# Tiny loads of 15 down to 3 rows behind one large load, in a two-layer decode kernel

## The chip, the core and the metric

The kernel runs on one core of a Trainium2 chip. The metric is the device time of one execution in microseconds (us). Before the change it is 1313.94 us, the median of three runs (1313.61 to 1314.49).

## The reference

Two rounds of the same two layers on an input `x` of 2 batches, 1 token and 448 features: attention against a cache of 4096 keys and values in 16 heads of 256, then a gated layer of 1792.

```
def _A_ref(x, k_cache, v_cache, wq, wo):
    q = heads(x @ wq)                                   # 2 x 16 x 1 x 256
    p = softmax(einsum("bhqd,bhkd->bhqk", q, k_cache) * 256 ** -0.5)
    return merge(einsum("bhqk,bhkd->bhqd", p, v_cache)) @ wo
def _B_ref(x, W_gate, W_up, W_down):
    gate = x @ W_gate; gate = gate * (gate > 0)
    return (gate * (x @ W_up)) @ W_down
x = x + _A_ref(layernorm(x), k_cache, v_cache, wq, wo)
x = x + _B_ref(layernorm(x), W_gate, W_up, W_down)
x = x + _A_ref(layernorm(x), k_cache, v_cache, wq, wo)  # the same caches and weights again
x = x + _B_ref(layernorm(x), W_gate, W_up, W_down)
```

Everything is float32. The keys and values are 134 MB each and are read in both rounds, so the kernel reads 560 MB.

## The kernel before

A *unit* is one pair of head and batch; there are 32, in the order `first` in the first round and `second` (the last four of `first` backwards, then the rest) in the second. For a unit VectorE (DVE) multiplies the 4096 keys with the query (L524) and sums each product (L538); GpSimd (POOL) takes the maximum and the sum over the partitions (L601, L629); ScalarE (ACT) takes the exponentials; TensorE (PE) weighs the values (L659) and projects (L711). Each of the 128 partitions holds 32 keys and 32 values of a unit.

All loads go into one tile, `arena`, which has room for three *blocks* of 64 KB a partition and three single places for weights. In the middle of each round a block is filled by one load of 128 x 16384 floats from `vk` (8.39 MB): the values of one unit and the keys of the next, which lie side by side in memory, 64 KB for each partition. Its size in the code is `n == PAIR`, and `WHOLE_FIRST` and `WHOLE_SECOND` are the positions in the two orders that are loaded so. Other positions are loaded in smaller parts, and between the blocks come pairs of weights (`w_pair`, 1.8 MB).

The list `pending` holds all loads in the order in which they are issued. `release` frees a place when a unit's keys or values have been used, and `pump` then issues from the head of the list whatever finds room. All these loads are issued on SyncE's (SP's) queue by one line (L159 before the change):

```
for i, j in zip(parts, parts[1:]):
    nc.sync.dma_start(dst[:, i:j], src[:, i:j])
```

The waits of each instruction are put in by the framework from the tiles that it reads and writes. Loads signal their landing on eight semaphores, `DMAHW0` to `DMAHW7`, which the loads take in turn; the input `x`, loaded on ACT's queue, has taken the first. SP works through its instructions in order.

Of the kernel before, what the change touches and what calls it, by code (L numbers as in the profile page):

```python
# [8 lines left out]
F32 = mybir.dt.float32  # L9
# [6 lines left out]
P = 128  # L16
# [7 lines left out]
PAIR = 2 * NC  # L24
# [2 lines left out]
KEPT = 20  # L27
ALONE = 25
SPARED = 12
TINY = 174  # L30
KEYS = 8
VALUES = 5
# [48 lines left out]
def two_layers(  # L81
# [10 lines left out]
    nc = tc.nc  # L92
    PSUM = bass.MemoryType.PSUM

    consts = ctx.enter_context(tc.tile_pool(name="consts", bufs=1))
# [20 lines left out]
    def source(key, n):  # L116
        kind, name, c = key
        if kind in "kv":
            h, b = name
            at = (h * B + b + (kind == "v")) % (H * B)  # L120
            if name in spared and n == PAIR:
                return vk[at, :, VALUES * DH : PAIR * UNIT - KEYS * DH]
            size = F if key in left_at else n * UNIT
            c += NC * (kind == "k" and n < PAIR)
            return vk[at, :, c * UNIT : c * UNIT + size]
        if kind == "g":
            return w_pair[name - 1]
        if key in parted:
            at = (kind == "q") * F
            return w_pair[0][:, at : at + F]  # L130
        if kind in "hqo":
            return w_head[weights.index(key)]
        if kind == "in":
            return w_in[:, c * F : (c + n) * F]
        return w_out[:, 14 * P * c : min(14 * P * (c + 1), 14 * D)]

    def pump(by_half=False):
        while pending:
            (kind, name, c), n = pending[0]
            last = at_of.get((kind, name, c - 1)) if kind in "kv" else None  # L140
            if kind == "g":
                last = MIDDLE - (name + 1) % 2
            at = units.take(n, kind, last)
            if at is None:
                return
            pending.pop(0)
            src = source((kind, name, c), n)
            assert at == left_at.get((kind, name, c), at)
            start = place(at) + VALUES * DH * (name in spared and n == PAIR)
            dst = arena[:, start : start + src.shape[1]]  # L150
            parts = [0, src.shape[1]]
            if by_half:
                parts[1:1] = [src.shape[1] // 2]
            if not pending:
                parts[1:1] = [src.shape[1] - CLOSE * TAIL]
            elif len(pending) == 1:
                parts[1:1] = [8 * P]
            for i, j in zip(parts, parts[1:]):
                nc.sync.dma_start(dst[:, i:j], src[:, i:j])  # L159
            for k in range(n):  # L160
                key = (kind, name, c + k)
                if n == PAIR:
                    key = ("k", name, k - NC) if k >= NC else ("v", behind[name], k)
                if kind == "g":
                    key = ("q", name, 0) if (name + k) % 2 == 0 else ("o", name - 1, 0)
                at_of[key] = at + k
                if kind == "in" and k:
                    lies_at[key] = start + k * F
            if n >= NC:
                blocks.add((kind, name))  # L170

    def place(at):
        packed = max(0, at - BLOCKS * PAIR)
        return at * UNIT - packed * (UNIT - F)
# [28 lines left out]
    def release(*key):  # L203
        if key in rest and key not in left_at:
            left_at[key] = at_of[key]
        units.free.add(at_of.pop(key))
        pump(key == ("k", second[0], 0))
# [57 lines left out]
    pending += of_second + [(("in", "", 0), 2)] + [(key, 1) for key in ffn_loads[2:]]  # L265

    tiny = consts.tile([P, TINY], F32, name="tiny")
    tiny_at = {}

    def little(name, *shape, bufs=2):  # L270

        n = 1
        for k in shape:
            n *= k
        if name not in tiny_at:
            start = tiny_at.get(None, 0)
            tiny_at[None] = start + n * bufs
            assert tiny_at[None] <= TINY
            tiny_at[name] = [tiny[:, start + n * i : start + n * (i + 1)] for i in range(bufs)]
        tiny_at[name].append(tiny_at[name].pop(0))  # L280
        found = tiny_at[name][-1]
        if len(shape) == 2:
            found = found.rearrange("p (i j) -> p i j", i=shape[0])
        return found
# [5 lines left out]
    y_end_row = extra[SUMS : SUMS + B, :TAIL]  # L290
    nc.scalar.dma_start(row[:B, :D], x.rearrange("b s d -> (b s) d"))
    pump()


# [5 lines left out]
    rows = little("rows", 4, bufs=1)  # L300
# [110 lines left out]
    def attention(order, after, q_first=None, begun=None):  # L411
# [86 lines left out]
        def score_block(u, c):  # L498
# [6 lines left out]
            there = [(kt, 0)]  # L505
            if order[u] == first[SPARED]:
                most = NT - KEYS
# [132 lines left out]
        def weigh(u, c):  # L640
# [5 lines left out]
            if c == 0:  # L646
                po_of[u] = po[u // 2 % 2]
            held = c == 0 and order[u] == first[SPARED - 1]
            if held and not ahead:
# [85 lines left out]
        for u in range(n_u + 2):  # L735
# [41 lines left out]
            if u == n_u - 1 and aside:  # L777
                units.free.add(slot)
                pump()
# [282 lines left out]
def build(nc, shapes):  # L1062
    import concourse.tile as _tile

    args = [
        nc.dram_tensor(f"in_{n}_dram", s, F32, kind="ExternalInput").ap() for n, s in shapes.items()
    ]
    for i, (shape, _) in enumerate(_OUTS):
        args.append(nc.dram_tensor(f"out_{i}_dram", shape, F32, kind="ExternalOutput").ap())
    with _tile.TileContext(nc) as tc:  # L1070
        two_layers(tc, *args)
# [12 lines left out]
```

## Time and profile before

| | |
|---|---|
| median of three runs | 1313.94 us |
| the profiled execution | 1314.3 us, of it 1312.0 us span |
| DVE busy | 1065.3 us (81%) |
| PE busy | 505.6 us (39%) |
| ACT, POOL busy | 195.2 us (15%), 297.9 us (23%) |
| SP's queue of loads | 560.48 MB, its packets took 99.5% of the time of 16 DMA engines |
| granted TensorE clock, mean | 0.69 |

The span runs from the first to the last instruction. An engine is busy while it computes; the queue of loads is busy while any of its packets is under way on the 16 DMA engines. A wait is put down to the work whose end released it. "SPq" is SP's own sequencer, where a load's row is the time that it takes to issue it, not to move it.

### The profile page before, as it was taken

The numbers are of one execution on the slowest core, as the hardware profiler recorded it, in microseconds if no ns is written. First come the engines' busy times: TensorE is split into PE (matmuls) and PEld (weight loads), VectorE is DVE, ScalarE is ACT, GpSimd is POOL, SyncE is SP. The second block draws the span as 40 slices with busy tenths as digits, with TensorE's granted clock in tenths as the row PEclk, the third lists the DMA queues.
The fourth block names the chain that finished last, engine by engine and source line by source line (L and its number), as shares of the span: only waits on it lengthen the run. The fifth ranks groups of instructions, "written<-read, shape, count | busy, mean of one in ns | idle before, by whom it ended". The sixth has DMA issues, their size and how long they took to land.

```text
span 1312.0 us, 8388 instructions
## 1 busy us (share of the span) xinstructions
PE 505.6 (39%) x3022; PEld 152.0 (12%) x3022; DVE 1065.3 (81%) x711; ACT 195.2 (15%) x789; POOL 297.9 (23%) x169
## 2 busy tenths in 40 slices
PE   3152243332433224324495445322342513433248
PEld 2010010000100001101141101100110100110013
DVE  4988988799897998787619896698999889886892
ACT  1100000010000000122417523000000100012231
POOL 0330412304123040021002151140345304100230
PEclk9665776657766577666697767666676666766669
DMA  9999999999999999999999999999999999999998
GB/s 408 438 432 432 434 426 438 438 426 434 434 430 432 438 432 424 443 420 429 422 399 421 434 427 439 438 436 430 423 443 432 430 430 438 432 432 427 429 421 337
DMA packets 20068, 561.00 MB, mean 428 GB/s; under 512 B 2232, under 2 KB 2364, under 8 KB 6844
## 3 DMA queue, kind: packets, MB, share of 16 engines
q1 hardware_dynamic: 20020, 560.48, 99.5%
q8 instruction: 23, 0.38, 0.1%
q14 instruction: 17, 0.14, 0.0%
q10 hardware_dynamic: 8, 0.00, 0.0%
HBM read 560.47 MB, written 0.00 MB: 427 GB/s over the span
## 4 chain that ended last, share of the span: by engine, by line
DMA 55%; DVE 31%; POOL 7%; PE 4%; issue 2%; ACT 1%; SPq 0%; POOLq 0%; DVEq 0%; ACTq 0%
DMA arena<-in_vk_dram 51%; DVE tiny L538 16%; DVE arena L524 10%; POOL tiny L629 4%; POOL tiny L601 4%; DMA arena<-in_w_in_dram 3%; DVE arena L573 2%; DVE arena L586 2%; DMA arena<-in_w_out_dram 1%; PE small L688 1%; PE po L453 1%; ACT arena L579 1%; DVE row L677 0%; DVE tiny L583 0%; ACT down L617 0%
## 5 line engine op out<-in xcount | busy, mean ns | idle before, releaser
L524 DVE TENSOR_TENSOR arena<-arena 128x8192 f32<-128x8192 f32 (+2 forms) x53 | 450.0, 8492 | 103.4 <-DMA arena<-in_vk_dram 102.6
L538 DVE TENSOR_REDUCE tiny<-arena 128x32 f32<-128x8192 f32 (+1 forms) x54 | 436.5, 8084 | 0.0
L659 PE MATMUL po<-arena,down 128*4 128x512 f32 x2052 | 313.2, 729 | 192.9 <-ACT down L617 116.5
L601 POOL PARTITION_ALL_REDUCE tiny<-tiny x63 | 121.0, 1920 | 719.2 <-DVE tiny L595 718.4
L688 PE MATMUL small<-tiny,row 128*128 128x2 f32 x128 | 30.9, 345 | 558.7 <-DVE row L677 558.7
L629 POOL PARTITION_ALL_REDUCE tiny<-tiny x63 | 149.0, 2364 | 60.4 <-ACT down L617 60.4
L613 ACT ACTIVATE tiny<-tiny 128x1 f32<-128x1 f32 x63 | 18.6, 295 | 734.6 <-POOL tiny L601 734.6
L659 PEld LDWEIGHTS po<-arena,down 128*4 128x4 f32 x2052 | 65.7, 97 | 410.5 <-issue 231.2
L688 PEld LDWEIGHTS small<-tiny,row 128*128 128x128 f32 x128 | 28.1, 306 | 589.1 <-DVE row L677 589.1
L453 PE MATMUL po<-arena,xs 128*33 128x512 f32 (+1 forms) x130 | 65.3, 661 | 0.0
L579 ACT ACTIVATE arena<-arena 128x256 f32<-128x256 f32 x135 | 54.4, 404 | 41.3 <-DVE arena L573 40.4
L711 PE MATMUL acc<-arena,tiny 128*2 128x448 f32 x128 | 51.0, 895 | 21.2 <-DVE tiny L701 21.1
L530 ACT ACTIVATE arena<-arena 128x256 f32<-128x256 f32 x112 | 44.8, 402 | 88.3 <-DVE arena L524 88.3
L465 POOL PARTITION_BROADCAST arena<-arena x32 | 21.8, 749 | 158.5 <-ACT arena L461 147.8
L573 DVE TENSOR_TENSOR arena<-arena 128x1024 f32<-128x1024 f32 (+2 forms) x21 | 32.8, 1560 | 3.4 <-PE acc L711 3.4
L677 DVE SCALAR_TENSOR_TENSOR row<-po,tiny,row 128x256 f32<-128x256 f32 x32 | 15.4, 480 | 22.1 <-ACT row L673 22.0
L461 ACT ACTIVATE arena<-po 33x512 f32<-33x512 f32 x13 | 7.7, 590 | 159.3 <-PE po L453 159.3
L701 DVE TENSOR_TENSOR tiny<-small,tiny 128x4 f32<-128x4 f32 x32 | 5.2, 161 | 28.6 <-PE small L688 28.6
L617 ACT ACTIVATE down<-tiny 128x32 f32<-128x32 f32 x64 | 26.6, 416 | 2.2
L579 ACT ACTIVATION_READ_ACCUMULATOR arena<-arena 128x1 f32 x135 | 25.2, 187 | 0.0
L453 PEld LDWEIGHTS po<-arena,xs 128*33 128x33 f32 x130 | 16.4, 136 | 62.1 <-issue 59.4
L530 ACT ACTIVATION_READ_ACCUMULATOR arena<-arena 128x1 f32 x112 | 21.0, 187 | 0.0
(174 smaller groups left out, 335.8 us busy)
## 6 DMA issues: line engine op xcount, KB each, us to landing
arena<-in_vk_dram SPq DMA_DIRECT2D x17, 4096.0 KB, 38.2
arena<-in_vk_dram SPq DMA_DIRECT2D x16, 2048.0 KB, 32.7
arena<-in_w_pair_dram SPq DMA_DIRECT2D x11, 1792.0 KB, 30.8
arena<-in_vk_dram SPq DMA_DIRECT2D x11, 1024.0 KB, 9.4
arena<-in_w_in_dram SPq DMA_DIRECT2D x12, 896.0 KB, 25.5
arena<-in_vk_dram SPq DMA_DIRECT2D x1, 6528.0 KB
arena<-in_w_head_dram SPq DMA_DIRECT2D x7, 896.0 KB, 22.0
arena<-in_w_out_dram SPq DMA_DIRECT2D x5, 896.0 KB, 19.6
```

What stands on the lines that cost most here:

```text
L453: nc.tensor.matmul(q[:, cols], xs[:, c, :], w_c, start=(i == 0), stop=(i == len(parts) - 1))
L524: nc.vector.tensor_mul(part, part, q_of[u][:, None, :].to_broadcast([P, n, DH]))
L530: nc.scalar.activation(kt[:, t, :], kt[:, t, :], AF.Copy, accum_out=s_of[u][:, t : t + 1])
L538: nc.vector.reduce_sum(found, part, axis=AX.X)
L573: nc.vector.tensor_mul(part[:, :whole, :], kt[:, :whole, :], q_of[u][:, None, :].to_broadcast([P, whole, DH]),)
L579: nc.scalar.activation(part[:, t, :], part[:, t, :], AF.Copy, accum_out=found[:, t : t + 1])
L601: nc.gpsimd.partition_all_reduce(mx_of[u], mx, P, RED.max)
L617: nc.scalar.activation(found, s_of.pop(u).rearrange("p (k r) -> p k r", r=2), AF.Exp, bias=nm, scale=sr[:, b : b + 1], accum_out=rs,)
L629: nc.gpsimd.partition_all_reduce(total[:, b : b + 1], rs, P, RED.add)
L659: nc.tensor.matmul(po_of[u][32 * t : 32 * t + 4, (i - 2 * t) * DH : (j - 2 * t) * DH], p_of[u][:, at : at + 4], values[:, i * DH : j * DH] ...
L688: nc.tensor.matmul(pT_of[u][:, c, :], row[:, c * P : (c + 1) * P], pick[:, b : b + B], start=True, stop=True,)
L711: nc.tensor.matmul(acc[at : at + B], oT_of[h][:, c, :], wo[:, c * D : (c + 1) * D], start=(n < 3), stop=(n >= n_u - 3),)
```

## The change

Behind a load of 128 x 16384 (or, for one unit in the second round, 128 x 13056) whose unit is listed in `STEPPED`, SP issues thirteen more loads. The first reads 15 rows of 13 floats, the next 14 rows of 12 and so on to 4 rows of 2, the last 3 rows of 14. They read the start of what the large load reads, and write side by side into a new tile `steps` of 104 floats a partition, which nothing reads.

```
+STEPS = {rows: rows - 2 if rows > 3 else 14 for rows in range(15, 2, -1)}
+STEPPED = [(2, 0), (6, 0), (10, 0), (13, 0)]
...
             for i, j in zip(parts, parts[1:]):
                 nc.sync.dma_start(dst[:, i:j], src[:, i:j])
+            if n == PAIR and name in STEPPED:
+                stairs(at, src)
...
+    def stairs(at, src):
+        start = 0
+        for rows, n in STEPS.items():
+            nc.sync.dma_start(steps[:rows, start : start + n], src[:rows, :n])
+            start += n
...
+    steps = consts.tile([P, sum(STEPS.values())], F32, name="steps")
```

The four units are loaded whole in the first round; in the second, of the four only (6, 0) and (10, 0) are (positions 16 and 24 of 9 to 28; (2, 0) is at 8 and (13, 0) at 30). That makes six places and 78 added loads: SP's queue has 140 rows before and 218 after. No instruction of another engine is added or moved. As `order` rows from here on, `arena<-in_vk_dram` is a load of keys and values, `DMAHW` are the eight semaphores of landings, and a semaphore named after an engine is that engine's progress.

SP's queue at the first place, the load of unit (2, 0), before. The first row is that load, the next three are the loads of the following units:

```order
L159 DMA arena<-in_vk_dram 128x16384 [waits DMAHW3_49,DVE_49,PE_49]
L159 DMA arena<-in_vk_dram 128x16384 [waits DMAHW0_49,DMAHW4_49,DVE_49,PE_49]
L159 DMA arena<-in_vk_dram 128x16384 [waits DMAHW1_49,DMAHW5_49,DVE_49,PE_49]
L159 DMA arena<-in_vk_dram 128x16384 [waits DMAHW7_49,DVE_49,PE_49]
L159 DMA arena<-in_w_pair_dram 128x3584 [waits PE_49,DMAHW6_49,Activation_49,Pool_49]
```

The same place now, from the same load (it is on `DMAHW7`, as the eighth load of the program) to the next load of a unit:

```order
L161 DMA arena<-in_vk_dram 128x16384 [waits DMAHW3_49,DVE_49,PE_49]
L181 DMA steps<-in_vk_dram 15x13 [waits DMAHW0_49]
...
L181 DMA steps<-in_vk_dram 10x8 [waits DMAHW5_49]
L181 DMA steps<-in_vk_dram 9x7 [waits DMAHW6_49]
L181 DMA steps<-in_vk_dram 8x6 [waits DMAHW7_49]
L181 DMA steps<-in_vk_dram 7x5 [waits DMAHW0_49]
L181 DMA steps<-in_vk_dram 6x4 [waits DMAHW1_49]
L181 DMA steps<-in_vk_dram 5x3 [waits DMAHW2_49]
L181 DMA steps<-in_vk_dram 4x2 [waits DMAHW3_49]
L181 DMA steps<-in_vk_dram 3x14 [waits DMAHW4_49]
L161 DMA arena<-in_vk_dram 128x16384 [waits DMAHW5_49,DVE_49,PE_49]
```

The next unit's load now stands thirteen loads further back, and the eighth tiny load (8x6) waits on the semaphore of the large load ahead of it.

SP's queue at the fifth place, unit (6, 0) in the second round, before:

```order
L159 DMA arena<-in_w_pair_dram 128x3584 [waits DMAHW6_49,PE_49,Pool_49]
L159 DMA arena<-in_vk_dram 128x13056 [waits DMAHW0_49,DVE_49,PE_49]
L159 DMA arena<-in_vk_dram 128x16384 [waits DMAHW1_49,DVE_49,PE_49]
L159 DMA arena<-in_vk_dram 128x16384 [waits DMAHW2_49,DVE_49,PE_49]
L159 DMA arena<-in_vk_dram 128x16384 [waits DMAHW4_49,DVE_49,PE_49]
```

The same place now, from the large load to the next:

```order
L161 DMA arena<-in_vk_dram 128x13056 [waits DMAHW4_49,DVE_49,PE_49]
...
L181 DMA steps<-in_vk_dram 11x9 [waits DMAHW5_49]
L181 DMA steps<-in_vk_dram 10x8 [waits DMAHW6_49]
L181 DMA steps<-in_vk_dram 9x7 [waits DMAHW7_49]
L181 DMA steps<-in_vk_dram 8x6 [waits DMAHW0_49]
L181 DMA steps<-in_vk_dram 7x5 [waits DMAHW1_49]
L181 DMA steps<-in_vk_dram 6x4 [waits DMAHW2_49]
L181 DMA steps<-in_vk_dram 5x3 [waits DMAHW3_49]
L181 DMA steps<-in_vk_dram 4x2 [waits DMAHW4_49]
L181 DMA steps<-in_vk_dram 3x14 [waits DMAHW5_49]
L161 DMA arena<-in_vk_dram 128x16384 [waits DMAHW6_49,DVE_49,PE_49]
```

Here too the eighth tiny load and the large load share a semaphore (the thirteenth, 3x14, and the fifth, 11x9, share `DMAHW5`, so the large load is on `DMAHW0`).

SP's queue near the end of the program, before. This piece is not touched by the change but for the numbers of its semaphores, and it is the place where the trace before shows such a wait by itself:

```order
L159 DMA arena<-in_vk_dram 128x4096 [waits DMAHW2_49]
L159 DMA arena<-in_vk_dram 128x4096 [waits PE_49]
L159 DMA arena<-in_vk_dram 128x4096 [waits DMAHW4_49,PE_49]
L159 DMA arena<-in_vk_dram 128x4096 [waits DMAHW5_49,DVE_49,Activation_49]
L159 DMA arena<-in_vk_dram 128x2048 [waits DMAHW6_49]
L159 DMA arena<-in_vk_dram 128x2048 [waits DMAHW7_49]
L159 DMA arena<-in_w_in_dram 128x3584 [waits DMAHW0_49,PE_49]
L159 DMA arena<-in_w_in_dram 128x1792 [waits DMAHW1_49]
L159 DMA arena<-in_w_in_dram 128x1792 [waits DMAHW2_49,PE_49]
```

The first and the last row are eight loads apart and name the same semaphore.

## The prediction

> **What bounds the kernel now.** I read the page's queues first, then stretches in the middle of the run, then SP's waits.
>
> ```profile
> span 1312.0 us, 8388 instructions
> ...
> GB/s 408 438 432 432 434 426 438 438 426 434 434 430 432 438 432 424 443 420 429 422 399 421 434 427 439 438 436 430 423 443 432 430 430 438 432 432 427 429 421 337
> DMA packets 20068, 561.00 MB, mean 428 GB/s; under 512 B 2232, under 2 KB 2364, under 8 KB 6844
> ...
> q1 hardware_dynamic: 20020, 560.48, 99.5%
> ...
> L524 DVE TENSOR_TENSOR arena<-arena 128x8192 f32<-128x8192 f32 (+2 forms) x53 | 450.0, 8492 | 103.4 <-DMA arena<-in_vk_dram 102.6
> ```
>
> One queue, SP's, is busy for 99.5% of the span. DVE, the busiest engine, still stands idle for 102.6 us ahead of its products, and what ends that is a landing. In the stages with large loads (columns: PE, PEld, DVE, ACT, POOL, then clock, DMA share, GB/s):
>
> ```profile
> 137.00:219.00 82.00, 26.86 (x154) 7.01 (x154) 71.52 (x19) 4.51 (x15) 20.16 (x10) 0.69 1.00 432
> 219.00:300.00 81.00, 29.69 (x156) 7.72 (x156) 71.07 (x20) 8.03 (x21) 20.15 (x10) 0.66 1.00 432
> 300.00:382.00 82.00, 27.57 (x154) 7.29 (x154) 71.18 (x19) 4.51 (x15) 20.56 (x10) 0.67 1.00 432
> ```
>
> The share is 1.00 and the rate 432 GB/s each time. So the loads bound the kernel: a load of 8.39 MB takes 8.39 / 0.432 = 19.4 us, and any time in which the queue is dry is added to the end. What keeps it from running dry is that SP issues early:
>
> ```profile
> 55.80 60.45 SPq L159 DMA_DIRECT2D arena<-in_vk_dram  x4
> DMA to landing us min/median/max: 42.5/42.5/42.5
> 75.00 43.34 DMA arena<-in_vk_dram
> 219.16 70.55 SPq L159 DMA_DIRECT2D arena<-in_vk_dram  x4
> DMA to landing us min/median/max: 43.3/43.3/43.3
> ```
>
> The first row is SP's timeline: the load of unit (2, 0), the first place, is issued at 55.80 us. The second, of that load alone, says that it lands 42.5 us later, at 98.3. The third, from the chain, is the load behind it, issued at 75.00 and landed at 118.3. So the next large load joins the queue 23 us before the one ahead has landed. The last two rows are the same for the second place: issued at 219.16, landed 43.3 us later.
>
> **What a load may wait for.** The added loads need a semaphore each, and the rows of the change name the one that each waits on. That such a wait holds SP until a landing is seen near the end of the run, in the chain and in SP's timeline:
>
> ```profile
> 1231.08 34.98 DMA arena<-in_vk_dram
> 1266.06 0.02 issue
> 1266.08 0.02 SPq L159
> 1266.10 0.03 issue
> 1266.12 28.27 DMA arena<-in_w_in_dram
> ...
> 1230.70 19.85 SPq L159 DMA_DIRECT2D arena<-in_vk_dram  x7
> 1256.34 10.11 SPq L159 DMA_DIRECT2D arena<-in_w_in_dram  x3
> ```
>
> The load issued at 1231.08 lands at 1266.06, and 0.06 us later SP issues another. By the two timeline rows the first is second of seven and the other third of the next three: eight loads later, the pair that shares `DMAHW2` in the order. The later load overwrites nothing of the earlier's; it waits because it takes its semaphore. So a load is not issued before the load eight places ahead of it has landed. With large loads in the middle of the run this costs nothing today: eight of them are over 100 us.
>
> **The change, step by step.** It removes and moves nothing; it adds 78 loads on SP's queue, thirteen at each of six places.
>
> *Tiny loads 1 to 7* wait on the loads ahead of the large one; the seventh waits on the landing of its direct forerunner. They then queue behind the large load. That holds SP some 20 us, but SP only holds up the next load, and see below.
>
> *Tiny load 8* waits on the landing of the large load itself, by both order pieces. SP reaches it long before and stands. When the large load lands, everything issued has landed but the seven tiny ones behind it: the queue is dry. The next large load, which before was under way already, is not yet issued. Its block was free 23 us ago, so it waits for nothing else.
>
> *From the landing to the next data.* SP goes on 0.06 us after the landing (row above). It issues tiny loads 8 to 13, six of them, then the large load. What one issue takes:
>
> ```profile
> 601.90 1.75 SPq L159 DMA_DIRECT2D arena<-in_vk_dram  x4
> L159 SPq DMA_DIRECT2D arena<-in_w_out_dram x10: 327/328/328, 670.8 to 1296.6; - x10
> 0.72 0.53 ACTq L291 DMA_DIRECT2D row<-in_x_dram  x1
> ```
>
> Four issued in a row take 1.75 us, 0.44 each. No row has one of 3 to 15 rows on SP; the nearest are the single issue of 0.33 us and ACT's two-row load of 0.53. I take 0.44, since it is SP's own row with issues back to back; ends 0.33 and 0.53. Six make 2.6 us (2.0 to 3.2). Loads 9 to 13 wait on 1 to 5, which land with the large load or shortly after it, so I count no more for them.
>
> Then the restart: from the issue into a dry queue until data flow. The trace has it at the very start:
>
> ```profile
> DMA to landing us min/median/max: 4.8/4.8/4.8
> ...
> 0.00:2.00 2.00, 0.00 (x0) 0.00 (x0) 0.06 (x1) 0.72 (x1) 0.39 (x5) 1.00 0.23 38
> 2.00:6.00 4.00, 0.00 (x0) 0.00 (x0) 0.00 (x0) 2.51 (x4) 0.00 (x0) 1.00 1.14 424
> ```
>
> The first load, 0.92 MB issued at 0.72 us, lands 4.8 us later; at 432 GB/s its data take 2.1, so the restart cost 2.7. By the stretches, 38 GB/s for 2 us and 424 for 4 moved 1.77 MB by 6.0 us, which is 4.1 us at 432: the restart cost 6.0 - 0.72 - 4.1 = 1.2. I take 2.0, in the middle, since the first way holds the spread of the 16 engines too and the second counts packets that are only begun. Sum for a place: 0.06 + 2.6 + 2.0 = 4.7 us; ends 0.06 + 2.0 + 1.2 = 3.3 and 0.06 + 3.2 + 2.7 = 6.0.
>
> The Trainium skill ("DMA: Bandwidth & Descriptors", Latency and other measured facts) puts the first byte of a load issued by SP at about 600 ns. With 0.6 in place of 2.0 a place would cost 3.3 us and the six 20. The rows above show more, 1.2 to 2.7, and I keep to them.
>
> *The tiny loads' own transfers* I cost at nothing: seven lie at the tail of the large load and six go while SP issues the next, all within the dry time. Without that cover they would be 117 rows of at most 56 bytes a place; no row prices one, but the gap bounds it.
>
> *Afterwards.* The load after next is issued in order right behind. Before, SP issued four loads from 55.80 to about 116 us, one in 20, so that one joined at about 95, shortly ahead of the large load's landing at 98.3; it now comes some 6 us late, into a queue that then holds 19 us of work. The dry time is not made up: the share was 1.00 already. DVE's work stays as it is and waits that much longer. The engines that finish the large load ahead of the others lose that lead too; it costs up to about 1 us in all, and is within the ends.
>
> *Sum.* Six places of 4.7 us are 28 us. The profiled execution took 1314.3 us, 2.3 around its span, and stands 0.4 us above the median of 1313.94, so one base serves both: 1314 + 28 = 1342 us. With the ends, 6 x 3.3 = 20 and 6 x 6.0 = 36: 1334 to 1350.
>
> **Rivals.** A measurement of this kernel can tell about 0.2%, 2.6 us, from no change.
>
> *SP is not held.* If the eighth wait is met by an older landing, or the added loads don't share the eight semaphores as the rows read, SP issues thirteen loads in 13 x 0.44 = 5.7 us, a quarter of its 23 us in hand. The time stays at 1314, or 1 to 2 us more for the transfers. Against it stand the 0.06 us between landing and issue above. For it: that is seen only with small loads. Chance 5%.
>
> *Not slower: the engines fall out of step.* Fewer rows than 16 in a load may reach some of the 16 engines and not others, so the stairs shift the engines against each other. If engines in step hinder one another at the memory, the rate rises afterwards. From 98 us on some 524 MB remain, 1213 us at 432 GB/s; to pay back 28 us the rate must reach 524 / 1.185 = 442 GB/s. At 443, the best slice of the page, the time is 1312. Against it: three stretches at 432 within one unit, and slices of 443 beside others of 420, which rows of 64 KB landing in one slice or the next explain. The Trainium skill (same page and section, on HBM row pitch at large powers of two) has such a rule: copies whose rows lie a large power of two apart fall to half their rate or less, perhaps by streams in step meeting in one channel. Here the pitch is 64 KB, below its cases, and no run here shows a rate that a shift has raised. Chance 3%, of which 2% faster and 1% the same.
>
> *The tiny loads land one after another.* If loads 1 to 5 land only after a restart each, 9 to 13 wait for them in turn: five times 1.2 to 2.7 us more a place, 36 to 81 us in all, 1378 to 1423. Nothing in the trace has a load waiting on a tiny one; but they were issued long before and only queue. Chance 2%.
>
> **How the numbers follow.** The dry queue at six places has 90%. Its ends, 1334 and 1350, come from restart and issue; I widen them by 2 us a side: above for the lead that the engines lose and for tiny loads that land late, below for a restart in mid-run that has less to bring up than the program's first load. The range 1332 to 1352 leaves out the rivals, 10%, and the outermost of its own case. Slower: 90% and the last rival's 2%, 92%. Same: 5% and 1%, 6%. Faster: 2%.
>
> **What would show it.** In the profile after, SP's queue of loads should fall from 99.5% to about 97.5% (28 us of 1340), with a stretch of some 5 us below full share behind each of the six large loads, the first near 98 us. SP should wait on `in_vk_dram` landings for some 20 us at each place, where it waited on DVE before, and its tiny loads should fall into two bunches, seven before the landing and six after, about 0.44 us apart. The next large load should be issued 2.7 us behind the landing and land 24 us behind it, not 20. DVE's idle time ahead of L524 should grow from 102.6 us by about 28. GB/s between the places should stay at 432. The forecast is wrong if SP runs through all thirteen before the landing, if the restart is under 1 or over 3 us, or if the rate between places moves.

## The result and the profile after

The changed kernel takes 1346.75 us, median of four runs (1346.52 to 1347.61), against 1313.91 us for the kernel before, measured beside it: a ratio of 1.0251 with a 95% interval of 1.0233 to 1.0268, 32.8 us slower. The profiled execution has a span of 1344.9 us, 32.9 more than before. In lines of the profile after, numbers of code lines are 2 higher in `pump` and 13 higher in the computation (L524 is now L537).

The page of the changed kernel, its rate by slice, its queue of loads and the wait of DVE ahead of its products:

```profile
span 1344.9 us, 8485 instructions
...
GB/s 409 429 367 437 427 435 437 370 406 443 423 437 398 405 427 437 342 433 432 423 412 421 431 426 439 437 431 435 431 345 437 429 437 430 374 433 431 417 424 350
...
q1 hardware_dynamic: 21424, 560.50, 97.3%
...
L537 DVE TENSOR_TENSOR arena<-arena 128x8192 f32<-128x8192 f32 (+2 forms) x53 | 450.0, 8492 | 140.4 <-DMA arena<-in_vk_dram 133.7
```

The bytes are the same but for 0.02 MB, the queue's share of the 16 engines' time falls from 99.5% to 97.3%, and DVE waits 31 us longer for landings. The rate is not lower everywhere: slices of 367, 370, 398 (with the 405 behind it), 342, 345 and 374 stand where the six places are, and most others are near what they were.

What SP waits for (in total, times, longest), the largest rows of the changed kernel:

```profile
SPq L161 <- DVE tiny L551: 578.6, 40, 35.9
SPq L181 <- DMA arena<-in_vk_dram: 214.7, 13, 19.2
```

SP waits for DVE some 250 us less than the 830.7 of before, and 214.7 us ahead of a tiny load until a load of keys and values lands: the large load of the place or, for the seventh tiny load, the one ahead of it. The first place, in SP's timeline and in the chain that ends with the product of the next unit:

```profile
56.55 0.33 SPq L161 DMA_DIRECT2D arena<-in_vk_dram  x1
...
98.48 1.94 SPq L181 DMA_DIRECT2D steps<-in_vk_dram  x6
100.53 0.83 SPq L161 DMA_DIRECT2D arena<-in_vk_dram  x2
```

```profile
56.55 41.91 DMA arena<-in_vk_dram
98.46 0.02 issue
98.48 0.27 SPq L181
98.75 0.04 issue
98.80 0.29 SPq L181
...
100.53 21.82 DMA arena<-in_vk_dram
122.35 0.02 issue
122.37 8.69 DVE arena L537
```

The large load lands at 98.46. SP issues the six remaining tiny loads from 98.48 on, one in 0.34 us, and at 100.53 the next large load, 25 us later than before. It lands at 122.35: 23.9 us behind the one ahead of it, where a load in a full queue takes 19.4. In between the queue stands dry (DMA share, then GB/s, in the last two columns):

```profile
98.50:100.50 2.00, 2.00 (x24) 0.54 (x24) 1.91 (x1) 0.07 (x1) 1.84 (x1) 1.00 0.03 4
```

### The profile page after: what moved, and what is told of

The parts are those of the page before. It is cut to its first block, busy times and chain, and to the rows that moved or that the text cites. A ratio compares the mean times of both kernels' runs of the same rounds, so it can differ in the third digit from the quotient of the medians.

```text
span 1344.9 us, 8485 instructions
## 1 busy us (share of the span) xinstructions
PE 509.5 (38%) x3022; PEld 154.1 (11%) x3022; DVE 1065.1 (79%) x711; ACT 195.3 (15%) x789; POOL 273.1 (20%) x169
## 3 DMA queue, kind: packets, MB, share of 16 engines
q1 hardware_dynamic: 21424, 560.50, 97.3%
## 4 chain that ended last, share of the span: by engine, by line
DMA 67%; DVE 23%; PE 5%; POOL 2%; issue 1%; ACT 1%; SPq 1%; DVEq 0%; POOLq 0%; ACTq 0%
DMA arena<-in_vk_dram 63%; DVE arena L537 10%; DVE tiny L551 10%; DMA arena<-in_w_in_dram 3%; DVE arena L599 1%; POOL tiny L642 1%; DMA arena<-in_w_out_dram 1%; PE po L466 1%; PE small L701 1%; DVE arena L586 1%; POOL tiny L614 1%; PE po L672 1%; SPq L181 1%; PE acc L724 1%; ACT arena L592 0%
## 5 line engine op out<-in xcount | busy, mean ns | idle before, releaser
L537 DVE TENSOR_TENSOR arena<-arena 128x8192 f32<-128x8192 f32 (+2 forms) x53 | 450.0, 8492 | 140.4 <-DMA arena<-in_vk_dram 133.7
L672 PE MATMUL po<-arena,down 128*4 128x512 f32 x2052 | 317.2, 736 | 186.4 <-ACT down L630 102.3
L614 POOL PARTITION_ALL_REDUCE tiny<-tiny x63 | 95.5, 1516 | 753.1 <-DVE tiny L608 752.5
L642 POOL PARTITION_ALL_REDUCE tiny<-tiny x63 | 149.6, 2374 | 60.4 <-ACT down L630 60.4
L724 PE MATMUL acc<-arena,tiny 128*2 128x448 f32 x128 | 51.1, 895 | 20.8 <-DVE tiny L714 20.7
L478 POOL PARTITION_BROADCAST arena<-arena x32 | 21.8, 749 | 181.0 <-ACT arena L474 170.1
L586 DVE TENSOR_TENSOR arena<-arena 128x1024 f32<-128x1024 f32 (+2 forms) x21 | 32.8, 1560 | 4.2 <-PE acc L724 4.2
```

The costliest lines, as they stand in the source:

```text
L537: nc.vector.tensor_mul(part, part, q_of[u][:, None, :].to_broadcast([P, n, DH]))
L586: nc.vector.tensor_mul(part[:, :whole, :], kt[:, :whole, :], q_of[u][:, None, :].to_broadcast([P, whole, DH]),)
L614: nc.gpsimd.partition_all_reduce(mx_of[u], mx, P, RED.max)
L642: nc.gpsimd.partition_all_reduce(total[:, b : b + 1], rs, P, RED.add)
L672: nc.tensor.matmul(po_of[u][32 * t : 32 * t + 4, (i - 2 * t) * DH : (j - 2 * t) * DH], p_of[u][:, at : at + 4], values[:, i * DH : j * DH] ...
L724: nc.tensor.matmul(acc[at : at + B], oT_of[h][:, c, :], wo[:, c * D : (c + 1) * D], start=(n < 3), stop=(n >= n_u - 3),)
```

## The experiments

All times are against runs of the kernel before on the same chip, whose medians were 1313.75 to 1314.04 us. Where a landing is named without a row, it is read from the trace's landing signals: the trace has 16 of them for each load of 128 rows, which I take to be one from each of the 16 DMA engines, and the last one ends the load.

**Where the wait begins: six tiny loads.** Only the first six of each place are kept:

```
-        for rows, n in STEPS.items():
+        for rows, n in list(STEPS.items())[:6]:
```

> Only the first six tiny loads of each place (15 to 10 rows; 36 of the 78). Theory A (the load that takes the large load's semaphore holds SP until it lands, and the queue runs dry if that load stands ahead of the next large one): the next large load is now the seventh behind and takes the semaphore of the load ahead of the large one, so nothing runs dry: 1314 us, within 2 us of before; queue of loads busy 99.4 to 99.5%. Rival B (each tiny load costs, whatever it waits for): 36/78 of 33 us are 15 us, 1329 us. Rival C (the shift of the engines against each other costs, or the first loads of it): between 1320 and 1347 us.

Measured: 1316.36 us, ratio 1.0019 (1.0010 to 1.0028), queue of loads 99.5% busy. The chain of this run at the first place shows what the next load now waits for:

```profile
40.12 38.91 DMA arena<-in_w_pair_dram
79.04 0.03 SPq L161
79.10 39.72 DMA arena<-in_vk_dram
```

It is the landing of the weights ahead of the large load, at 79.0 us; the load behind is issued 0.1 us later, with the large one still queued in front. Nothing runs dry, as theory A has it. The 2.5 us are slightly more than the 2 allowed. They are not such a wait: behind four of the six places the next load lands 0.25 to 0.33 us further behind the one ahead than in the trace before. Spread over the 36 loads the 2.5 us are 0.07 each, which the queue pays when it has no gap to hide them in (below).

**And one more: seven.** The same edit with `[:7]`.

> One more than in the run of six: the first seven tiny loads (15 to 9 rows; 42 of the 78). Theory A: the next large load is the eighth behind and waits for the large load's landing, so the queue runs dry for wait and restart, without the six issues of 0.34 us: about 0.1 + 2.4 = 2.5 us at each place where the full stairs had 4.6 to 5.5; 15 us and the lost lead of the engines (4 to 5 us in all): 1332 to 1336 us. A step of some 19 us from six to seven loads. Rival B (by the number of loads): 42/78 of 33 us are 18 us, 1332 us, but then six loads give 1329 and the step is 3 us.

Measured: 1334.19 us, ratio 1.0154 (1.0140 to 1.0168). One more load at each place, of 9 rows and 7 floats, costs 17.8 us, where the first six cost 2.5: rival B, a price for each load, falls. The chain at the second place of this run gives the restart by itself, since no tiny load is issued in the gap:

```profile
222.43 43.31 DMA arena<-in_vk_dram
265.75 0.03 SPq L161
265.82 21.88 DMA arena<-in_vk_dram
```

The next load is issued 0.08 us behind the landing and takes 21.9 us, so 2.5 more than in a full queue. And the six issues that distinguish this run from the changed kernel cost 1346.75 - 1334.19 = 12.6 us, 0.35 for each of the 36, which is their spacing in the chain.

**All thirteen, but never against a dry queue.** Six behind the large load, six behind the next load on the queue, one behind the third:

```
             if n == PAIR and name in STEPPED:
-                stairs(at, src)
+                left[:] = list(STEPS.items())
+                begun[0] = 0
+            if left:
+                stairs(src)
...
+        for rows, n in left[:6]:
...
+        del left[:6]
```

> All thirteen tiny loads at each place, but six behind the large load, six behind the next and one behind the one after. Theory A: the load that waits for a landing now has a large load queued ahead of it; the queue does not run dry: 1314 to 1316 us (at the fourth place a small load of weights alone covers the wait, up to 1 us). Rivals B and C (number of loads, or shift of the engines): 1340 to 1347 us, as with the change.

Measured: 1318.91 us, ratio 1.0039 (1.0027 to 1.0052), queue 99.3% busy. The same 78 loads of the same shapes cost 5.0 us instead of 32.8, so neither their number nor a shift of the engines against each other makes the loss. SP's timeline at the first place:

```profile
56.70 0.33 SPq L161 DMA_DIRECT2D arena<-in_vk_dram  x1
57.07 17.69 SPq L186 DMA_DIRECT2D steps<-in_vk_dram  x6
78.82 0.36 SPq L161 DMA_DIRECT2D arena<-in_vk_dram  x1
98.25 2.03 SPq L186 DMA_DIRECT2D steps<-in_vk_dram  x6
100.39 0.35 SPq L161 DMA_DIRECT2D arena<-in_vk_dram  x1
```

Six loads still wait for the large one's landing at 98.2, but the next large load has been issued at 78.8 and flows meanwhile. Only at the fourth place is the cover thin, since the load that flows meanwhile is one of weights of 0.9 MB; the load behind that one comes 0.3 us late. The 5.0 us missed the expectation of up to 2: 78 loads at 0.064 us each on average, about the price with 36. Here the tiny transfers have no gap to hide in.

**More places.** The stairs also behind the unit after each of the four, so that six of seven new places follow directly on an old one:

```
-STEPPED = [(2, 0), (6, 0), (10, 0), (13, 0)]
+STEPPED = [(2, 0), (2, 1), (6, 0), (6, 1), (10, 0), (10, 1), (13, 0), (13, 1)]
```

> The full stairs at thirteen places instead of six: behind the same units and behind the unit after each, in both rounds where these are loaded whole; six of the seven new places are the very next large load, one stands alone. Theory A with the dry queue of 4.6 us at each place and a lost lead that costs only where some time has passed since the last place: 13 x 4.6 = 60 us and 5 to 6 us for the lead: 1379 to 1381 us. Rival D (a place costs 5.5 us wherever it stands, restart and all): 13 x 5.47 = 71 us, 1385 us.

Measured: 1380.79 us, 66.9 more than before, within what theory A gave and 4 us below rival D. DVE's timeline shows the starts of its products, each within 0.15 us of a landing, at the second place and its new neighbour:

```profile
272.39 8.76 DVE L537 TENSOR_TENSOR arena<-arena 128x6144 f32<-128x6144 f32 x2 [4.55 <-DMA arena<-in_vk_dram]
296.41 8.69 DVE L537 TENSOR_TENSOR arena<-arena 128x8192 f32<-128x8192 f32 x1 [6.32 <-DMA arena<-in_vk_dram]
320.86 8.69 DVE L537 TENSOR_TENSOR arena<-arena 128x8192 f32<-128x8192 f32 x1 [5.28 <-DMA arena<-in_vk_dram]
```

Two products in a row start 24.0 and 24.5 us after the one ahead, 4.6 and 5.1 late. Restarts add up and none is made good.

**The shape.** All added loads of 128 rows instead of 15 down to 3:

```
-            nc.sync.dma_start(steps[:rows, start : start + n], src[:rows, :n])
+            nc.sync.dma_start(steps[:, start : start + n], src[:, :n])
```

> Thirteen added loads at the same six places, of the same 13 down to 2 and 14 floats, but of all 128 rows each, so that no part of the 16 engines gets more of them. Theory A (the wait and the restart): the shape is no part of it; the issues take 0.34 to 0.44 us each instead of 0.34: 1346 to 1351 us. Rival C (the shift of the engines by fewer rows costs): back toward 1340 us or below.

Measured: 1352.11 us, ratio 1.0288 (1.0273 to 1.0303), 1 us over the range given. The shape costs a little, by the issue: SP's timeline has the six in the gap of this run in 2.70 us where the stairs take 1.94.

```profile
98.51 2.70 SPq L181 DMA_DIRECT2D steps<-in_vk_dram  x6
101.32 0.84 SPq L161 DMA_DIRECT2D arena<-in_vk_dram  x2
```

0.76 us more at six places are 4.6 of the 5.4 us. Stairs are thus no worse than even loads, and rival C falls a second time.

**The lost lead.** The restart and the issues, 4.5 us at a place, leave some 4 to 5 of the 32.8 us open. In the changed kernel one of the loads after a place lands about 1.2 us late by itself. DVE's timeline at the second place:

```profile
267.79 8.76 DVE L537 TENSOR_TENSOR arena<-arena 128x6144 f32<-128x6144 f32 x2 [4.56 <-DMA steps<-in_vk_dram]
291.61 8.69 DVE L537 TENSOR_TENSOR arena<-arena 128x8192 f32<-128x8192 f32 x1 [6.11 <-DMA arena<-in_vk_dram]
312.38 8.69 DVE L537 TENSOR_TENSOR arena<-arena 128x8192 f32<-128x8192 f32 x1 [1.60 <-DMA arena<-in_vk_dram]
331.75 8.69 DVE L537 TENSOR_TENSOR arena<-arena 128x8192 f32<-128x8192 f32 x1 [1.73 <-DMA arena<-in_vk_dram]
```

The steps are 23.8 us (the place), 20.8 and 19.4. In the stretch of the 20.8 the list of queues has a row that the next stretch lacks, one packet of 16 KB of instructions on another queue:

```profile
q8 instruction: 1, 0.02, 0.3%
```

Theory E: the packet takes one of the 16 DMA engines for about 1 us. If that engine has a lead on the slowest, nothing shows; behind a place all engines start level, so the first such packet makes its engine the last.

The landing signals show these leads. In the trace before, the 16 signals of the load behind the second place lie 2.8 us apart, and a packet at 288.2 us leaves the next landing in its time, 19.36 us behind the one ahead. In the changed kernel they lie 0.6 us apart there, and 2.0 at the next landing, the late one, with the packet at 293.5 us ahead of it.

To move the packets, unread products were added on TensorE at the start of the changed kernel; first 64:

```
     add_rows(B, ident[:, :B], start=True)
+    for _ in range(64):
+        busy(1)
     attention(first, keep)
```

> The changed kernel with 64 unread products on TensorE at the start (128 more instructions, some 4 us of TensorE in a stretch where it waits for loads). The time should stay: 1345 to 1350 us. It is about the lost lead. Theory E (a load after a place lands about 1.2 us late because one engine fetches 16 KB of instructions meanwhile): these fetches come by count of TensorE's instructions, some 4 a us, so each comes about 30 us earlier: the one at 138.6 us near 107, and the late landing moves from the second large load behind the first place (20.5 us behind the first, now 19.4) to the first one (23.9 us behind the place's own load, now 24.9 to 25.2). Rival F (the restart itself puts one engine back, on whatever load): the late landings stay where they are.

Measured: 1346.71 us. There is one more packet in all (24 for 23), but for a few the rest kept their times, and the late landings mostly stayed too. The expectation had counted 128 more instructions; the page has 256 (3150 matmuls and as many weight loads, for 3022 of each), and they made just one packet, so most others stayed where they were. One did move: behind the third place the packet at 487.0 us came at 512.7, and the late landing went with it, from 500.9 to 524.3 us, one load on. The control, the kernel before with the same products:

> The kernel before with the same 64 unread products at the start, as a control for the run before it: the loads bound it and TensorE has room: 1313 to 1316 us.

Measured: 1316.67 us, ratio 1.0019 (1.0009 to 1.0028), 0.7 us above the range given. Its trace shows why it is slower: here, without any tiny load, a large load was issued too late. SP waited 17.4 us for TensorE's weighing of the values (L659), which began at 295.4 us and not at 282.8 as before; what made it late was not followed further. SP's timeline has the issue, and the stretch ahead of it has an empty queue (the last two columns are DMA share and GB/s):

```profile
301.81 0.33 SPq L159 DMA_DIRECT2D arena<-in_vk_dram  x1
```

```profile
299.00:301.00 2.00, 2.00 (x16) 0.32 (x8) 0.00 (x0) 0.00 (x0) 0.00 (x0) 0.55 0.00 0
```

The load lands at 323.91, 22.1 us behind its issue. A queue that runs dry for another reason thus costs its restart too, 2.7 us here, in a kernel without tiny loads. The 16 signals, 2.8 us apart before, lie 0.9 apart at this landing, and the next packet (349.1 us) is followed by a landing 1.0 us late, as theory E has it.

Since 64 products made just one packet, 32 were taken next:

> As the run before it on this question, with 32 unread products instead of 64. The 64 added just one fetch and left nearly all others at their times, so 64 were one block of 16 KB and 32 are half of one. Theory E: the fetches now fall about midway between those of the changed kernel (70.4, 138.6, 191.3, 293.5, 348.2, 427.3, 487.0 us): near 105, 165, 245, 320, 390, 457. So behind the first place the late landing moves from the second large load to the first (fetch near 105), behind the second place to the second or third load (fetch near 320), behind the third from the third to the first (near 457). Rival F (the restart itself): they stay at the second, second and third load. The time stays within 2 us of 1346.7.

Measured: 1346.66 us. DVE's timeline at the second place of this run:

```profile
267.89 8.76 DVE L537 TENSOR_TENSOR arena<-arena 128x6144 f32<-128x6144 f32 x2 [4.86 <-DMA steps<-in_vk_dram]
291.66 8.69 DVE L537 TENSOR_TENSOR arena<-arena 128x8192 f32<-128x8192 f32 x1 [6.07 <-DMA arena<-in_vk_dram]
311.01 8.72 DVE L537 TENSOR_TENSOR arena<-arena 128x8192 f32<-128x8192 f32 x1 [0.18 <-DMA arena<-in_vk_dram]
331.71 8.69 DVE L537 TENSOR_TENSOR arena<-arena 128x8192 f32<-128x8192 f32 x1 [2.74 <-DMA arena<-in_vk_dram]
```

Now the steps are 23.8, 19.4 and 20.7: the late landing has moved one load on, and the row of the instruction packet has moved with it, out of the stretch from 291.6 to 312.4 us and into that from 312.4 to 331.7. The landing signals lie 0.5, 0.5 and 1.9 us apart at the three landings. This place came out as expected. At the first the packet came at 99.6 us, into the gap, and the late landing at 185.8 with the next packet (179.0), not at the first load. At the third it was expected near 457 us and came at 438, in the gap, and the late landing followed with the next packet, at 522.6. So the places were foretold in one case of three, but in each the late landing went where the packet went: rival F, a fixed after-effect of the restart, falls. The total stays, since each stretch between places still holds a packet.

## Why the prediction was right, and where it was off

The forecast was 1342 us, range 1332 to 1352, slower at 92%; measured were 1346.75.

- **The eighth load holds SP until the large one lands, and the queue runs dry.** Right. Six loads cost 2.5 us and seven 20.3; the wait stands in the rows of SP with 214.7 us.
- **Six issues of 0.44 us, 2.6 in all.** High: they take 2.05 us, 0.34 each. The row taken had loads of 128 rows; with those in the gap the same six take 2.70. The price that came closest was the single issue of 0.33 us, though its loads had 128 rows too; ACT's load of two rows, the nearest in number of rows, was the furthest off with 0.53.
- **A restart of 2.0 us.** Low within its ends: 21.8 - 19.4 = 2.4 us in the chain after, 2.5 in the run of seven, up to 2.8 at the other places. Of the two ways to read it off the program's start, the landing (2.7) was nearer than the stretches (1.2). The Trainium skill's 600 ns to the first byte ("DMA: Bandwidth & Descriptors", Latency and other measured facts) is a fourth of what the restart costs a large load here.
- **4.7 us a place, 28 in all.** From the landings, the load behind each place comes 4.5, 4.6, 4.5, 5.0, 4.9 and 4.5 us later than the 19.36 us of a full queue: 28.1 us. That the sum is so close is luck: the two errors above cancel.
- **The lead that the engines lose, up to about 1 us in all.** This is the term that was mis-sized. The rest, 32.8 - 28.1 = 4.7 us, is its size: late landings of 0.9 to 1.4 us in the stretches behind the places, less some 2 us of late landings that only the kernel before has (its load behind the first place took 20.0 us, for one). The prediction counted only the lead that is there when the queue runs dry. What it missed is that the lead has been hiding the instruction packets, and that a restart exposes one again. It read the 99.5% as one queue; it is 16 engines, and the last sets the landing.
- **The tiny transfers at nothing, in the gap.** Right for the change: by the trace's packets, at the first place the last tiny one ends at 101.06 us, and the next load's first packet begins at 101.50. Without the gap they cost 0.064 to 0.07 us each, as two runs show, so the rival "SP is not held" would have ended near 1319, not 1314 to 1316.
- **The rivals.** That the engines out of step would run faster is not borne out: a large load in a full queue takes 19.36 us in both traces, and even loads of 128 rows lose as much and more. The Trainium skill's rule on row pitch ("DMA: Bandwidth & Descriptors", Latency and other measured facts) has the rate halved at pitches of 4 and 8 MiB; at the 64 KB here no run shows such an effect.
- **The signs in the profile.** The share was to fall to 97.5% (97.3), DVE's wait to rise by about 28 us (31), the next load to be issued 2.7 us behind the landing (2.07) and to land 24 behind it (23.9). The rate between the places was to stay; it does, but for the late landings.

## What to carry to other kernels

On a queue that bounds the kernel, a load's price is not its bytes but what it waits for: count how many loads ahead the semaphore it takes was last used, and see that the next large load is issued before that one lands. With eight semaphores in turn, six small loads in a row between two large ones were nearly free here and seven were not. Small loads that must go there are better spread between large ones: the same 78 cost 5 us instead of 33.

## What the runs showed of the hardware that was not expected

- Issuing one of several small loads takes SP 0.34 us with 3 to 8 rows and 0.47 us with 128, by the spacing in the gaps.
- A queue that has run dry costs a large load 2.4 to 2.8 us from its issue, beyond its 19.4 us; at the first place its first packet begins 1.0 us behind the issue (101.50 for 100.53).
- A packet of 16 KB of TensorE's instructions takes one DMA engine for about 1 us (0.3% of 16 engines in 20.8 us). Behind a restart, with the landing signals 0.5 to 0.9 us apart, it delays a landing by 0.8 to 1.4 us in these runs; with 2.8 us between them the packet at 288.2 us in the trace before delays none.
